# Turning the result blocks back on VectorE for every batch, in a fused attention and mixer kernel

## The chip, the cores and the metric

The kernel runs on one core of a Trainium2 chip, in one launch. The metric is the device time of one execution in microseconds. Engines are named as the profile names them: PE (TensorE; PEld is its weight load), DVE (VectorE), ACT (ScalarE), POOL (GpSimd) and SP (SyncE, which here only issues DMAs). Each engine works through its own instructions in the order in which the program issues them.

## The reference

Two blocks in a row, all in float32. Attention with 8 batches, 8 heads, 576 positions and 64 columns a head keeps only the 32 largest scores of each row; the mixer then works on x of shape (8, 576, 512).

```python
def _attn_ref(q, k, v):
    scores = scale * np.matmul(q, k.transpose(0, 1, 3, 2))
    kth = np.partition(scores, -32, axis=-1)[..., -32:-31]
    scores = np.where(scores >= kth, scores, -1000000000.0)
    attn = np.exp(scores - np.max(scores, axis=-1, keepdims=True))
    attn = attn / (np.sum(attn, axis=-1, keepdims=True) + 1e-09)
    return np.matmul(attn, v)

def _moe_ref(x, U, V, w_ch1, w_ch2):      # x: the heads side by side
    h = x.transpose(0, 2, 1) @ U @ V
    u = x + h.transpose(0, 2, 1)
    return u + np.maximum(u @ w_ch1, 0.0) @ w_ch2
```

## The kernel before

**Attention.** Two heads form a pair; a batch has four pairs, and a pair is worked through in five chunks of query rows: four of 128 rows for each head, and one with the last 64 rows of both heads. A step `n` of the main loop stands for one chunk. `scores` (matmul L323, copies L351) runs one step ahead. `front` finds the 32 largest scores of each row on DVE: in rounds of MAX8 (L432, L436, L446, L463) and MATCH_REPLACE8 (L434, L458), which remove the eight largest each time. The first part of `front`, up to L446, is issued at the start of the step by `next(fronts[n])`; a later `next(here)` issues the first L458, and so on. ACT and POOL put the threshold into the scores (L485, L488, L491), and ACT takes the exponentials (L397).

The probabilities must be transposed before they meet v. From the middle of the second batch `blocks` does that: DVE turns 32x32 blocks (L518, tile `y`, one buffer), four DMAs take them to DRAM (L524, tile `away`), and a fifth brings them back in transposed order (L528, tile `PT`). `values` reads `PT` two steps later in L585. A smaller part goes through PE (L551). `load` fetches the next pair with 21 DMAs on SP (L247, L252, L276, L279, L280), and DVE turns it (L293).

**Mixer.** `mixed` makes `uT`, the transposed u of a batch, pair by pair. With the last pair of a batch it appends the generator `mlp(b)` to `fillers`. `mlp` goes over the 576 positions in two spans, of 320 and 256 columns. In each span the first layer runs over 16 blocks of hidden units (L656, Relu L668), the second over four blocks `c` of 128 output channels (L675, 16 matmuls each). The sum with u lands in `oT`, transposed: 128 channels by 320 or 256 positions. ACT copies it from PSUM (L690) and POOL adds u (L691); in the last batch DVE does both at once (L688).

**Order.** The order is written by hand (`manual_schedule`). `fill`, called eight times a step, takes as many matmuls from `fillers` as a share of work says (`due`). So the mixer of batch b runs between the attention steps of batch b + 1, and the mixer of the last batch runs alone at the end.

**Turning back.** `mlp` appends `turned_back(...)` for each `c` to the list `late` and calls it later: at the 13th matmul of the next `c` (`f == 12`), at the fifth block of the next span's first layer (`f == 4`), or, for the last one of the batch, when the generator is resumed after its last yield. The function has two ways. One turns `oT` with PE transposes into PSUM (L723), copies with ACT (L725, L727), and writes with one DMA (L729), or two where the span has the last 64 positions (L734). The other turns 32x32 blocks with one DVE instruction (L705) into the tile `ob` (two buffers), and writes each quarter of 32 channels with a DMA for each of the position groups (L710 twice, L715 where the span has the last 64 positions): 12 DMAs in the first span, 8 in the second. It writes pieces of 32 floats, 128 bytes; the first way writes pieces of 512 bytes. The second way is now taken in the last batch alone, and there not for the very last block.

Of the kernel before, what the change touches and what calls it, by code (L numbers as in the profile page):

```python
# [26 lines left out]
def kernel(  # L27
# [29 lines left out]
    B, H, S, D = q.shape  # L57
# [4 lines left out]
    NF, NC = F // P, C // P  # L62
# [32 lines left out]
    SPAN = ((0, 2 * P + TAIL), (2 * P + TAIL, S))  # L95
# [30 lines left out]
    def rows(t):  # L126
        return P if t < NT else TAIL
# [568 lines left out]
    def turned_back(b, chunks, lo, c, oT):  # L696


        def run():
            cs = slice(c * P, (c + 1) * P)  # L700
            if b == B - 1 and (lo, c) != (SPAN[1][0], NC - 1):

                w = sum(rows(t) for t in chunks)
                ob = mlpp.tile([P, 3 * P], F32, tag="ob", name="ob", bufs=2)
                nc.vector.transpose(ob[:, 0:w], oT[:, 0:w])  # L705
                for a in range(4):
                    cs = slice(c * P + a * BLK, c * P + (a + 1) * BLK)
                    ba = ob[a * BLK : (a + 1) * BLK]
                    for t in chunks[0:2]:
                        nc.sync.dma_start(  # L710
                            out[b, 0:MAIN, cs].rearrange("(m i t) c -> t i m c", i=BLK, t=NT)[t],
                            ba[:, OFF[t] - lo : OFF[t] - lo + P].rearrange("i (m c) -> i m c", c=BLK),
                        )
                    if NT in chunks:
                        nc.sync.dma_start(  # L715
                            out[b, MAIN:S, cs].rearrange("(m i) c -> i m c", i=BLK),
                            ba[:, 2 * P : 2 * P + TAIL].rearrange("i (m c) -> i m c", c=BLK),
                        )
                return
            tp = ps_t.tile([P, 3, P], F32, tag="tp", name="tp")  # L720
            for i, t in enumerate(chunks):
                n = rows(t)
                nc.tensor.transpose(tp[0:n, i, :], oT[:, OFF[t] - lo : OFF[t] - lo + n], ident)  # L723
            ob = mlpp.tile([P, 3, P], F32, tag="ob", name="ob", bufs=2)
            nc.scalar.copy(ob[:, 0:2], tp[:, 0:2, :])  # L725
            if NT in chunks:
                nc.scalar.copy(ob[0:TAIL, 2], tp[0:TAIL, 2, :])  # L727
            t = chunks[0]
            nc.sync.dma_start(  # L729
                out[b, 0:MAIN, cs].rearrange("(p t) c -> p t c", t=NT)[:, t : t + 2, :],  # L730
                ob[:, 0:2],
            )
            if NT in chunks:
                nc.sync.dma_start(out[b, MAIN:S, cs], ob[0:TAIL, 2])  # L734

        return run
# [195 lines left out]
```

## Time and profile before

| | |
|---|---|
| median of 3 runs | 1718.03 us (1717.31 to 1718.37) |
| the profiled execution | 1716.65 us, span in the profile 1714.9 us |
| granted TensorE clock, mean | 0.97 |
| busy, share of the span | PE 94%, DVE 87%, ACT 60%, POOL 55% |
| PE transposes of `oT` (L723) | 142, mean duration 273 ns |
| block transposes of `oT` on DVE (L705) | 7, 445 to 513 ns |
| DMAs to the output | 57 L729, 28 L734; 56 L710, 16 L715 |

The span falls in four parts. Up to about 300 us PE is less than full, with the first batches' exact top-32 search on DVE and the weights still arriving; up to about 400 us DVE is full; from there to 1561 us attention and mixer run together in a pattern that comes back every 193.8 us; the rest is the end of the second-to-last mixer and the last mixer on PE. A row of busy times counts overlapping instructions once. In a row of instructions the mean duration of a pipelined matmul is longer than the time by which it holds up the next one. An idle time is given in brackets with what ended it.

### The profile page before, as it was taken

To read this page: it belongs to the slowest core of one execution; us is meant where nothing else is said; L and a number is where in the kernel's file an instruction comes from. 1 tells how busy PE (TensorE), PEld (TensorE's weight loads), DVE (VectorE), ACT (ScalarE), POOL (GpSimd) and SP (SyncE) were. 2 spreads that over 40 slices of the span, in tenths; PEclk is the share of its full clock that TensorE was granted. 3 is DMA by queue.
4 is the path that set the end of the run, shared out by engine and by line. 5 is a ranking of instruction groups with operands and counts; after the bars stand their busy time and mean duration, and the time that the engine had idled before them with its cause. 6 is when DMAs were issued, how large, how long until landed. Compare 5 with 4: busy or idle time off the path is not lost.

```text
span 1714.9 us, 29637 instructions
## 1 busy us (share of the span) xinstructions
PE 1613.5 (94%) x9489; PEld 1219.8 (71%) x9489; DVE 1484.2 (87%) x4317; ACT 1023.3 (60%) x2582; POOL 944.9 (55%) x749
## 2 busy tenths in 40 slices
PE   4666799998999999999999999999999999999999
PEld 2444566787777877788677877788677877788777
DVE  7999989999999999999999999999999999992000
ACT  4888797665656556565656566565655566563100
POOL 4778578666555555565555555565555555552000
PEclk7777899999999999999999999999999999999999
DMA  3322322344444444444444444444444444432010
GB/s 87 95 84 84 84 78 61 77 123 122 108 112 112 117 117 106 112 116 114 115 109 111 119 112 108 114 113 114 111 108 120 118 108 114 106 93 71 3 16 13
DMA packets 275837, 167.37 MB, mean 98 GB/s; under 512 B 173920, under 2 KB 260192, under 8 KB 275680
## 3 DMA queue, kind: packets, MB, share of 16 engines
q1 hardware_dynamic: 274624, 165.20, 37.2%
q8 instruction: 75, 1.23, 0.3%
q14 instruction: 82, 0.67, 0.1%
q10 hardware_dynamic: 1056, 0.26, 0.1%
HBM read 101.42 MB, written 63.96 MB: 96 GB/s over the span
## 4 chain that ended last, share of the span: by engine, by line
PE 71%; DVE 19%; SPq 3%; ACT 2%; issue 2%; DMA 2%; POOL 1%; POOLq 0%; DVEq 0%; ACTq 0%
PE mm L656 27%; PE mm L675 21%; PE sc L323 8%; DVE upper L458 6%; PE O L585 6%; DVE m L463 6%; DVE first L446 2%; SPq L252 2%; PE tp L551 1%; PE O L571 1%; SPq L247 1%; PE up L631 1%; PE O L581 1%; PE tp L546 1%; DVE y L518 1%
## 5 line engine op out<-in xcount | busy, mean ns | idle before, releaser
L675 PE MATMUL mm<-hT,w 128*128 128x256 f32 (+1 forms) x2048 | 529.5, 407 | 0.0
L656 PE MATMUL mm<-uT,w 128*128 128x256 f32 (+1 forms) x2048 | 522.8, 407 | 0.0
L491 POOL TENSOR_TENSOR Ssb<-Ssb,E 128x576 f32<-128x576 f32 x271 | 379.2, 1417 | 246.2 <-ACT E L488 245.8
L656 PEld LDWEIGHTS mm<-uT,w 128*128 128x128 f32 x2048 | 380.0, 191 | 97.6 <-issue 2.6
L675 PEld LDWEIGHTS mm<-hT,w 128*128 128x128 f32 x2048 | 377.9, 191 | 93.0 <-issue 2.9
L463 DVE MAX8 m<-upper 128x8 f32<-128x304 f32 (+1 forms) x864 | 407.7, 508 | 3.6
L458 DVE MATCH_REPLACE8 upper<-m,upper 128x304 f32<-128x304 f32 (+1 forms) x576 | 285.7, 502 | 0.0
L390 POOL TENSOR_TENSOR lower<-Ssb 128x576 uint32<-128x576 uint32 (+1 forms) x135 | 174.3, 1291 | 147.2 <-ACT Ssb L351 51.0
L393 POOL TENSOR_TENSOR lower<-lower,upper 128x576 uint32<-128x576 uint32 (+1 forms) x135 | 174.3, 1291 | 112.2 <-DVE upper L392 104.7
L397 ACT ACTIVATE Ssb<-Ssb,nmax 128x576 f32<-128x576 f32 x286 | 221.5, 777 | 15.3 <-POOL Ssb L468 9.3
L668 ACT ACTIVATE hT<-mm 128x320 f32<-128x320 f32 (+1 forms) x256 | 105.1, 410 | 192.9 <-PE mm L656 191.0
L323 PE MATMUL sc<-qkT 64*128 64x288 f32 x1334 | 211.7, 441 | 8.6 <-ACT Ssb L358 7.8
L488 ACT ACTIVATE E<-Ssb,least 128x576 f32<-128x576 f32 x271 | 198.0, 769 | 5.2
L323 PEld LDWEIGHTS sc<-qkT 64*128 64x128 f32 x1334 | 116.3, 183 | 63.8 <-issue 24.2
L585 PE MATMUL O<-PT,va 128*64 128x128 f32 x2048 | 144.5, 285 | 3.3 <-DMA PT<-away 3.2
L518 DVE STREAM_TRANSPOSE y<-Ssb 128x512 f32<-128x512 f32 x208 | 134.5, 682 | 14.8 <-ACT Ssb L397 14.7
L351 ACT COPY Ssb<-sc 128x576 f32<-128x576 f32 x216 | 127.5, 643 | 32.6 <-PE sc L323 31.0
L688 DVE TENSOR_TENSOR oT<-uT,mm 128x320 f32<-128x320 f32 (+1 forms) x8 | 3.6, 454 | 144.5 <-PE mm L675 144.5
L585 PEld LDWEIGHTS O<-PT,va 128*64 128x64 f32 x2048 | 113.2, 140 | 19.7 <-DMA PT<-away 3.9
L432 DVE MAX8 upper<-lower 128x8 f32<-128x288 f32 x243 | 97.9, 439 | 23.2 <-POOL lower L393 21.2
L392 DVE TENSOR_TENSOR upper<-sc,Ssb 128x576 f32<-128x576 f32 (+1 forms) x135 | 92.0, 682 | 20.7 <-ACT Ssb L351 20.1
L458 DVE MATCH_REPLACE8 upper<-first,upper 128x304 f32<-128x304 f32 x243 | 109.8, 458 | 0.0
(91 smaller groups left out, 1878.7 us busy)
## 6 DMA issues: line engine op xcount, KB each, us to landing
away<-y SPq DMA_DIRECT2D x416, 128.0 KB, 2.4
PT<-away SPq DMA_DIRECT2D x104, 512.0 KB, 3.3
raw<-in_moe_w_ch_dram SPq DMA_DIRECT2D x32, 512.0 KB, 3.9
va<-in_v_dram SPq DMA_DIRECT2D x64, 128.0 KB, 2.2
out_dram<-ob SPq DMA_DIRECT2D x57, 128.0 KB, 2.0
ld<-in_q_dram SPq DMA_DIRECT2D x108, 64.0 KB, 2.6
ld<-in_k_dram SPq DMA_DIRECT2D x108, 64.0 KB, 2.3
ld<-in_q_dram SPq DMA_DIRECT2D x108, 8.0 KB, 2.2
```

Source lines behind the costliest of these rows:

```text
L323: nc.tensor.matmul(out, lhsT=qkT[half(h), 0, cols(t)], rhs=qkT[half(h), 1, lo:hi], start=True, stop=True,)
L390: nc.gpsimd.tensor_tensor(bottom, a.bitcast(U32), b.bitcast(U32), ALU.add)
L393: nc.gpsimd.tensor_tensor(bottom, bottom, top.bitcast(U32), ALU.subtract)
L397: nc.scalar.activation(E, chunk, AF.Exp, bias=nmax, scale=SCALE, accum_out=total)
L458: nc.vector.match_replace(nxt, ms[c], curs[c], NEG)
L463: nc.vector.max(ms[c], curs[c])
L488: nc.scalar.activation(gap, chunks[c], AF.Relu, bias=least[:, c : c + 1], scale=-WIDEN)
L491: nc.gpsimd.tensor_tensor(chunks[c], chunks[c], gap, ALU.subtract)
L518: nc.vector.transpose(y[:, :, h].rearrange("p r c j -> p c r j"), E2[:, a : a + MAIN].rearrange("p (c r j) -> p c r j", c=NT, r=4),)
L585: nc.tensor.matmul(O[half(h)], lhsT=va[:, h, j, :], rhs=PB[:, h, j] if shared(g, t) else PT[:, NT * h + j], start=False, stop=(j == NT - 1),)
L656: nc.tensor.matmul(ph[:, 0:w], lhsT=w1[:, cc, f * P : (f + 1) * P], rhs=uT[:, cc, lo:hi], start=(cc == 0), stop=(cc == NC - 1),)
L675: nc.tensor.matmul(po[:, 0:w], lhsT=w2[:, f, c * P : (c + 1) * P], rhs=hTs[f][:, 0:w], start=(f == 0), stop=(f == NF - 1),)
```

## The change

One condition in `turned_back`. The way over DVE is taken for every block of every batch, apart from the very last block of the last batch, which keeps the way over PE.

```diff
         def run():
             cs = slice(c * P, (c + 1) * P)
-            if b == B - 1 and (lo, c) != (SPAN[1][0], NC - 1):
+            if (b, lo, c) != (B - 1, SPAN[1][0], NC - 1):

                 w = sum(rows(t) for t in chunks)
                 ob = mlpp.tile([P, 3 * P], F32, tag="ob", name="ob", bufs=2)
                 nc.vector.transpose(ob[:, 0:w], oT[:, 0:w])
                 for a in range(4):
                     ...
                     for t in chunks[0:2]:
                         nc.sync.dma_start(...)
                     if NT in chunks:
                         nc.sync.dma_start(...)
                 return
             tp = ps_t.tile([P, 3, P], F32, tag="tp", name="tp")
```

`oT` is made as before: by ACT and POOL in the first seven batches, by DVE in the last.

## The prediction

> **What bounds the kernel now.** I read the page first, then busy time by windows. From about 400 us on the order repeats every 193.8 us, one batch. Columns: window, length, then busy us (count) of PE, PEld, DVE, ACT, POOL, granted clock, DMA share, GB/s.
>
> ```profile
> 304.00:434.00 130.00, 123.69 (x772) 97.78 (x769) 129.45 (x405) 80.12 (x208) 77.40 (x62) 0.97 0.42 109
> 970.00:1164.00 194.00, 192.73 (x1164) 147.17 (x1164) 184.42 (x565) 118.33 (x304) 111.90 (x89) 1.00 0.44 113
> ```
>
> In the steady batches PE is busy 192.73 of 194 us and DVE 184.42. PE's waits there (582 to 1551 us) are one line, once per batch:
>
> ```profile
> PE tp L723 <- POOL oT L691: 6.4, 5, 1.3
> ```
>
> So PE sets the pace, and the only thing it waits for is the last turn-back of a batch. In 304 to 434 it is the other way round: DVE has no gap (129.45 of 130) and PE waits for what DVE delivers. After 1561 us DVE has nothing left and PE sets the end alone.
>
> **What leaves PE.** I call one `run()` of `turned_back` a turn: 56 turns change, eight per batch (0 to 3 of three PE transposes, 4 to 7 of two), 140 transposes. Their price is not the row's mean (273 ns, pipelined), but the shift of the next matmul, in PE's timeline:
>
> ```profile
> 1087.46 0.49 PE L723 MATMUL tp<-ident,oT 128*128 128x128 f32 x3
> 1087.79 1.51 PE L675 MATMUL mm<-hT,w 128*128 128x320 f32 x5
> ...
> 1010.30 0.60 PE L675 MATMUL mm<-hT,w 128*128 128x256 f32 x2
> 1012.17 0.44 PE L723 MATMUL tp<-ident,oT 128*128 128x128 f32 x2 [1.27 <-POOL oT L691]
> 1012.45 1.78 PE L656 MATMUL mm<-uT,w 128*128 128x320 f32 x6
> ```
>
> Three transposes take 1087.79 - 1087.46 = 0.33 us, 0.11 each. Turn 7 holds L656 from 1010.73 (second L675 plus its 0.215 pitch) to 1012.45: 1.7 us. A steady batch frees 4 x 0.33 + 3 x 0.22 + 1.7 = 3.7 us of PE. ACT loses 56 copies of 0.373 and 28 of 0.258 us, 28 us in all; at 118 of 194 us it is not the bound and PE waits nowhere for it in a steady batch, so I count nothing (were ACT the cover of some stall that is due, this would be a gain of up to that stall).
>
> [...]
>
> **What DVE gets.** The last batch shows the price: L705 takes 445 to 513 ns, so a batch adds 4 x 0.51 + 4 x 0.45 = 3.8 us, and 184.4 + 3.8 = 188.2 fits under PE's new 190.1. But DVE is in order. A step starts with `next(fronts[n])` (up to L446); turn 7 comes in a `fill()` behind scores and L551, before `next(here)` issues L458. So the new transpose stands between L446 and L458, and its data are late:
>
> ```profile
> 1006.47 0.83 DVE L446 MAX8 first<-upper 128x8 f32<-128x304 f32 x2
> 1007.23 0.07 DVE L458 MATCH_VALUE_LOAD upper<-first,upper 128x8 f32 x1
> ...
> 1012.51 0.69 DVE L518 STREAM_TRANSPOSE y<-Ssb 128x512 f32<-128x512 f32 x1
> 1016.02 0.71 DVE L518 STREAM_TRANSPOSE y<-Ssb 128x512 f32<-128x512 f32 x1 [2.82 <-ACT Ssb L397]
> ...
> 1011.39 0.73 POOL L691 TENSOR_TENSOR oT<-oT,uT 128x256 f32<-128x256 f32 x1 [0.22 <-DVE upper L458]
> ```
>
> oT is there at 1012.12, DVE wants it at 1007.23. With 0.5 us of its own, DVE goes on at 1012.6, 5.4 us late. Queued behind are two rounds of MATCH_REPLACE8 and MAX8, then y (L518). Y's second half had waited 2.82 us for ACT; that gap swallows part, so y ends at 1013.8 + 5.4 = 1019.2 instead of 1016.7, 2.5 late. Y goes out and comes back as PT through SP (L524, L528), and L585 reads it:
>
> ```profile
> 1020.58 0.34 SPq L528 DMA_DIRECT2D PT<-away  x1
> 1025.67 1.09 PE L585 MATMUL O<-PT,va 128*64 128x128 f32 x16
> ```
>
> With the page's 3.3 us to landing PT is there at 1023.9, 1.8 us early. It will come 2.5 later and PE will ask 1.7 earlier: a stall of 2.4 us. The other seven turns find oT ready (turn 0: DVE at 1083.7, POOL done at 1079) and cost their 0.5 us, beneath gaps such as L392's 1.66 us.
>
> **What SP gets.** One or two DMAs per turn become 12 (turns 0 to 3) or 8. In the last batch 12 of them run from 1630.81 to 1636.57: 5.7 us, 0.475 each; 8 take 3.8. A batch adds 80 x 0.475 = 38 us of SP and removes 12 issues of 0.55, 7. Before, SP issues in the window 64 L524 at 0.43, 64 loads at 0.62, 16 L528 at 0.34, 20 for v at 0.54 and 12 outputs: 90 us, 8 between them, and waits 31 for away to land (L528). The sum goes from 129 to 160 of 194. In order, though, a burst delays what follows. The worst place is turn 3, behind a head pair's 21 loads:
>
> ```profile
> 1137.54 0.63 SPq L280 DMA_DIRECT2D vt<-in_v_dram  x1
> 1138.27 1.44 SPq L729 DMA_DIRECT2D out_dram<-ob  x1
> 1139.81 0.49 SPq L734 DMA_DIRECT2D out_dram<-ob  x1
> 1140.49 1.89 SPq L524 DMA_DIRECT2D away<-y  x4
> 1144.44 0.34 SPq L528 DMA_DIRECT2D PT<-away  x1
> 1152.88 1.09 PE L585 MATMUL O<-PT,va 128*64 128x128 f32 x16
> ```
>
> Turn 2's burst comes before the block ahead (away at 1120.5, burst over at 1122.3), so the loads start 1.8 late and end at 1140.0; the burst ends at 1145.7. Away is 5.2 us late against a margin of 1152.88 - 1144.44 - 3.3 = 5.1, and PE has gained 1.3: a stall of 1.4 us. The same sum at turn 0 (away 1091.0 to 1095.4; margin 1104.5 - 1095.0 - 3.3 = 6.2) and turn 1 (1102.3 to 1105.9; margin 5.1) leaves about 1 us each; turns 4 to 6 push by 3 at most against 6 to 7. Two buffers are asked in time: `ob` is free again when the burst two turns earlier has landed (10 us before at the least), and `y`, with one buffer, when away has landed, at turn 1 by 1110.0 for a y at 1110.6; half a microsecond more and DVE waits for what is over. The pieces shrink from 512 bytes to 128: in the last batch's bursts the DMA share is 0.14 to 0.18 beside 0.44 in a steady batch, and each lands in 1.5 us, so I charge only 0.3 us per batch for later landings. Its bounds: zero, and 2 us at each of the four blocks a batch with under 2.5 us to spare.
>
> [...]
>
> **The sum.** Steady batches (1 to 5): -3.7 + 2.4 + 1.4 + 0.3 = +0.4, five times: +2.0.
>
> Batch 0 turns back from 296 to 423. There DVE is the bound, so turns 1 to 3 lengthen the path by 3 x 0.53 = 1.6. Turn 3's burst (from 347.4) pushes away, PT and then the loads from 355.1 to 358.5; they landed at 367.0 for a DVE that took them at 368.2, so DVE loses some 0.7 more. PE takes over at 397.55, 2.3 late. It gains 0.7 at turns 4 to 6 and 2.4 at turn 7 (its wait of 2.14 and the pair), and loses 0.5 on a block that turn 5's burst makes late. DVE, 3.8 late with turns 4 to 6, comes to turn 7 at 422.4 (L446 was done at 418.6), finds oT at 424.2, goes on at 424.7, and y is 5.7 late where PE has 1.2 to spare (PT issued at 440.0, L585 at 444.4) and is itself 0.25 early: a stall of 4.7. In all 2.3 - 0.7 - 2.4 + 0.5 + 4.7 = +4.4; bounds 0 (all in slack) and +9 (each term twice).
>
> Batch 6: turns 0 to 3 free 1.3 us, but the last PT lands at 1561.0, just as L585 starts, so PE only waits longer there. Turns 4 to 7 lie behind it: 6 x 0.11 + 1.5 = 2.2 us gained. Tail unchanged.
>
> Sum: 2.0 + 4.4 - 2.2 = +4.2 on 1716.65, the profiled execution (span 1714.9 plus 1.75 outside): 1720.9. The median of the runs is 1.4 higher, 1718.03, so 1722.2.
>
> **Rivals.** *PE keeps its gain.* The bursts stay in their margins and batch 0 costs 2: 5 x (-3.7 + 2.4) + 2 - 2.2 = -6.7, 1711. For it: DMA share 0.44, margins of 5 to 7 us behind loads. Against: the margins at turns 1 and 3 come out at 1 us or none. Without any stall it would be 7 x 3.7 = -26, 1692; the L446/L458 order excludes that.
>
> *SP becomes the bound*, the case that is clearly slower. Place: second layer of the first span, 55 us a batch with four bursts of 5.7. It decides when away and PT land 1 us later each: blocks with 1.6 to 2.4 us to spare then stall by some 1 us, four a batch, 4 x 6 batches = 24 on the small case, 1742. For it: PT landings up to 5.4 us in the trace. Against: the last batch's bursts land in 1.5 us at a 0.18 share.
>
> *DVE as the bound*: 188.2 + a 5 us wait at turn 7 = 193, nothing spare; gaps that do not close add 1 us a batch, +5 on the forecast, 1727, inside the range.
>
> **How the numbers follow.** Forecast (losses at turn 7 and turn 3 eat the gain) 0.54, PE keeps its gain 0.24, SP 0.22. A measurement of this kernel tells about 0.2% (3.4 us) from no change. The forecast's +4.2 lies just past that: of its 0.54 I put 0.33 slower, 0.19 within, 0.02 faster; of the second 0.20 faster, 0.04 within; the third is slower. That is 0.22, 0.23 and 0.55. The range 1710 to 1740 cuts off the far ends of both rivals.
>
> **What would show it.** L723 down to 2 per run, PE's L723 wait gone; DVE idle 3 to 5 us before L705 once a batch, by POOL oT L691; new PE waits of 1 to 2.5 us, L585 on PT, once or twice a batch; period near 194. Wrong if PE waits nowhere (then 1711 or less), or if L585 waits at four or more blocks a batch.

## The result and the profile after

The changed kernel takes 1739.68 us (median, 1737.49 to 1741.05) against 1718.19 for the kernel before on the same chip: a ratio of 1.0125, 95% interval 1.0107 to 1.0142. It is slower. The profiled execution took 1739.59 us, 22.9 more than the one before, with a span of 1737.4. PE is busy 92% of the span instead of 94%, DVE 87% as before. The times further down are medians of a run's executions; in two of the runs one execution was far longer than the others of the same kernel (2127.3 and 5579.27 us), and it is left out.

I measure the pattern at the L585 that follows turn 7, which stands once in every batch. Before, it starts at 444.4, 638.2, 831.9, 1025.7, 1219.4 and 1413.2 us, 193.8 apart. After, at 452.05, 648.7, 846.3, 1046.9, 1241.5 and 1437.0: periods of 196.6, 197.6, 200.7, 194.5 and 195.5. So the 22.5 us by which the span grew are 7.7 up to the end of batch 0, 16.1 in batches 1 to 5, and -1.3 behind them. The windows of the changed kernel, three whole batches (columns as in the prediction):

```profile
846.00:1047.00 201.00, 194.77 (x1142) 148.09 (x1143) 187.83 (x575) 115.53 (x293) 112.06 (x89) 0.97 0.44 109
1047.00:1241.00 194.00, 190.22 (x1140) 145.20 (x1140) 185.98 (x572) 114.93 (x292) 111.31 (x88) 1.00 0.46 113
1241.00:1437.00 196.00, 190.28 (x1142) 145.28 (x1142) 187.44 (x574) 115.47 (x293) 111.94 (x89) 1.00 0.45 112
```

Two things are to be seen. PE's work is down to 190.2 where the granted clock is 1.00, but the windows are 4 to 6 us longer than that: PE waits. And in the longest one PE is busy 4.5 us more with as many instructions, at a granted clock of 0.97: it runs slower for part of the time. The table of waits, 434 to 1570 us, has PE's only line and the first of DVE's (us in total, times, longest):

```profile
PE O L585 <- DMA PT<-away: 27.7, 17, 3.3
DVE ob L705 <- POOL oT L691: 16.2, 5, 3.3
```

PE's L723 wait is gone. L585 waits for PT instead, and DVE waits 3.2 us once a batch for the `oT` of turn 7. The timeline at one turn 7, with DVE, POOL, SP and PE one below the other:

```profile
1028.78 0.84 DVE L446 MAX8 first<-upper 128x8 f32<-128x304 f32 x2
1032.86 0.45 DVE L705 STREAM_TRANSPOSE ob<-oT 128x256 f32<-128x256 f32 x1 [3.24 <-POOL oT L691]
...
1038.49 1.29 DVE L518 STREAM_TRANSPOSE y<-Ssb 128x512 f32<-128x512 f32 x2
...
1032.10 0.72 POOL L691 TENSOR_TENSOR oT<-oT,uT 128x256 f32<-128x256 f32 x1 [0.22 <-ACT oT L690]
...
1031.41 7.80 SPq L710 DMA_DIRECT2D out_dram<-ob  x16
1039.80 1.75 SPq L524 DMA_DIRECT2D away<-y  x4
1043.70 0.34 SPq L528 DMA_DIRECT2D PT<-away  x1
...
1046.94 1.09 PE L585 MATMUL O<-PT,va 128*64 128x128 f32 x16 [2.20 <-DMA PT<-away]
```

DVE is done with L446 at 1029.6 and stands until POOL has made `oT` at 1032.8; y (L518), away and PT come late by it, and PE stands 2.2 us. SP is through with the bursts of turns 6 and 7 at 1039.2, before y is ready at 1039.78, so here DVE sets the time and not SP.

The other place is turn 3, behind the 21 loads. SP, then PE, and below them the DVE instruction that makes y, in the last of the steady batches:

```profile
1332.69 0.90 SPq L710 DMA_DIRECT2D out_dram<-ob  x2
...
1338.42 1.83 SPq L524 DMA_DIRECT2D away<-y  x4
1342.35 0.34 SPq L528 DMA_DIRECT2D PT<-away  x1
1342.74 0.63 SPq L247 DMA_DIRECT2D ld<-in_q_dram  x1
...
1349.92 1.43 SPq L252 DMA_DIRECT2D ld<-in_k_dram  x1
...
1356.50 0.64 SPq L280 DMA_DIRECT2D vt<-in_v_dram  x1
1357.24 1.11 SPq L710 DMA_DIRECT2D out_dram<-ob  x2
...
1362.66 0.43 SPq L715 DMA_DIRECT2D out_dram<-ob  x1
1363.19 2.20 SPq L524 DMA_DIRECT2D away<-y  x4
1367.38 0.34 SPq L528 DMA_DIRECT2D PT<-away  x1
...
1370.62 1.09 PE L585 MATMUL O<-PT,va 128*64 128x128 f32 x16 [2.93 <-DMA PT<-away]
...
1354.13 1.28 DVE L518 STREAM_TRANSPOSE y<-Ssb 128x512 f32<-128x512 f32 x2
```

Turn 2's burst (from 1332.69) pushes the away of the block ahead, that pushes the loads, turn 3's burst (1357.24 to 1363.1) comes behind them, and only then the four L524. DVE had y ready at 1355.4. Away starts 7.8 us later, and PE stands 2.93 us.

The third thing is the clock. Rows of 3.41 us each, as long as the half clock from 847.18 to 850.59 in them; the second number is the length, the third PE's busy time, and behind those of the five engines stands the granted clock:

```profile
843.77:847.18 3.41, 1.44 (x20) 1.09 (x18) 3.38 (x10) 0.98 (x2) 2.45 (x2) 1.00 0.48 162
847.18:850.59 3.41, 3.41 (x15) 2.02 (x12) 3.41 (x13) 1.71 (x4) 0.51 (x2) 0.50 0.58 146
850.59:854.00 3.41, 3.41 (x14) 2.38 (x14) 3.41 (x13) 1.34 (x3) 1.94 (x2) 1.00 0.73 195
1045.11:1048.52 3.41, 1.58 (x20) 1.35 (x22) 3.41 (x11) 1.25 (x3) 2.35 (x2) 1.00 0.58 182
1048.52:1051.93 3.41, 3.41 (x17) 2.26 (x14) 3.41 (x14) 1.71 (x4) 1.41 (x1) 1.00 0.36 98
```

The first row holds the stall of 1.98 us that ends at 846.26. In the row behind it PE is full but the granted clock is 0.50: 1.7 us of work lost. The fourth row holds the stall of 2.20 us that ends at 1046.94, and in the row behind it the clock is 1.00. Between 452 and 1437 us the changed kernel has three such stretches of 3.4 us and one of 6.8, each at the end of a stall of L585: 8.5 us lost. One more follows the stall that ends at 1437.0. The kernel before has none between 434 and 1570.

With that the account closes, batch by batch: -3.7 freed, plus the stalls (4.9, 5.6, 6.0, 4.3, 5.2), plus the half clock (1.7, 1.7, 5.1, 0, 0) gives +2.9, +3.6, +7.4, +0.6, +1.5; measured are +2.9, +3.8, +6.9, +0.8, +1.7.

### The profile page after: what moved, and what is told of

Its sections match the earlier page's. It is cut to its first block, busy times and chain, and to the rows that moved or that the text cites. A ratio compares the mean times of both kernels' runs of the same rounds, so it can differ in the third digit from the quotient of the medians.

```text
span 1737.4 us, 29816 instructions
## 1 busy us (share of the span) xinstructions
PE 1606.6 (92%) x9349; PEld 1211.1 (70%) x9349; DVE 1505.4 (87%) x4373; ACT 1001.2 (58%) x2498; POOL 944.6 (54%) x749
## 4 chain that ended last, share of the span: by engine, by line
PE 56%; DVE 28%; DMA 6%; SPq 4%; ACT 2%; POOL 2%; issue 2%; DVEq 0%; POOLq 0%
PE mm L675 21%; PE mm L656 18%; DVE upper L458 9%; DVE m L463 8%; PE sc L323 7%; PE O L585 5%; DMA PT<-away 3%; DVE first L446 3%; DVE lower L434 2%; DMA away<-y 2%; DVE upper L436 1%; DVE y L518 1%; DVE upper L432 1%; PE tp L551 1%; SPq L247 1%
## 5 line engine op out<-in xcount | busy, mean ns | idle before, releaser
L675 PE MATMUL mm<-hT,w 128*128 128x256 f32 (+1 forms) x2048 | 523.9, 407 | 0.0
L458 DVE MATCH_REPLACE8 upper<-m,upper 128x304 f32<-128x304 f32 (+1 forms) x576 | 285.9, 503 | 0.0
L323 PE MATMUL sc<-qkT 64*128 64x288 f32 x1334 | 216.5, 449 | 8.4 <-ACT Ssb L358 7.5
L585 PE MATMUL O<-PT,va 128*64 128x128 f32 x2048 | 145.9, 286 | 35.9 <-DMA PT<-away 35.8
L585 PEld LDWEIGHTS O<-PT,va 128*64 128x64 f32 x2048 | 114.0, 141 | 53.7 <-DMA PT<-away 26.2
L518 DVE STREAM_TRANSPOSE y<-Ssb 128x512 f32<-128x512 f32 x208 | 134.8, 684 | 10.2 <-ACT E L488 4.0
L594 ACT COPY XT<-O 128x128 f32<-128x128 f32 x128 | 33.9, 265 | 153.4 <-PE O L585 153.3
L458 DVE MATCH_REPLACE8 upper<-first,upper 128x304 f32<-128x304 f32 x243 | 109.9, 459 | 0.0
L434 DVE MATCH_REPLACE8 lower<-upper,lower 128x288 f32<-128x288 f32 x243 | 106.0, 443 | 0.0
```

The lines of the kernel that those rows point to most:

```text
L323: nc.tensor.matmul(out, lhsT=qkT[half(h), 0, cols(t)], rhs=qkT[half(h), 1, lo:hi], start=True, stop=True,)
L458: nc.vector.match_replace(nxt, ms[c], curs[c], NEG)
L518: nc.vector.transpose(y[:, :, h].rearrange("p r c j -> p c r j"), E2[:, a : a + MAIN].rearrange("p (c r j) -> p c r j", c=NT, r=4),)
L585: nc.tensor.matmul(O[half(h)], lhsT=va[:, h, j, :], rhs=PB[:, h, j] if shared(g, t) else PT[:, NT * h + j], start=False, stop=(j == NT - 1),)
L675: nc.tensor.matmul(po[:, 0:w], lhsT=w2[:, f, c * P : (c + 1) * P], rhs=hTs[f][:, 0:w], start=(f == 0), stop=(f == NF - 1),)
```

## The experiments

The first theory is the prediction's: two separate costs, turn 7's place in DVE's order and SP's bursts, each a stall of PE, to which the half clock is added. Its rivals: DVE's added work limits; the pieces of 128 bytes limit; or batch 0's late start is what matters.

**Turn 7 alone is moved.** The last turn of a batch is called after the step's last L458, not before its first.

```diff
-        late.pop()()
+        held.append(late.pop())
...                                # in the step, after the last next(here)
+        while held:
+            held.pop(0)()
```

> Only the last turn of each batch (turn 7) is moved: it is issued at the end of the step, after y, instead of between L446 and L458. DVE still does all turns, SP still writes the bursts. Theory (each steady batch loses a stall of 2 to 2.6 us at the block behind turn 7, one of 2.2 to 3.3 at the block behind turn 3's burst, and 1.7 us at half clock after some of these, against 3.7 gained): DVE's wait in front of L705 (16.2 us from 434 to 1570) is gone, so is PE's stall of 2 us at the block after it, five times, one of 1.3 in batch 0, and about half of the clock dips: 12 to 17 us less than the changed kernel, 1723 to 1728. Rival (DVE's or SP's total work sets the period, the place of the wait does not matter): 1737 to 1741. The stall behind turn 3's burst stays in both.

Measured: 1720.11 us, ratio 1.001 (1.000 to 1.002), 3 us below my range. PE's wait, and the window of a batch:

```profile
PE O L585 <- DMA PT<-away: 16.5, 10, 2.9
801.00:996.00 195.00, 191.42 (x1140) 146.04 (x1136) 186.86 (x572) 115.23 (x293) 111.41 (x89) 0.99 0.45 112
```

The stall behind turn 7 is gone in every batch (PT is there 1.2 to 1.4 us before L585). What is left is the one behind turn 3, 2.6 to 2.9 us each, and half clock behind four of those five. DVE does the same work as in the changed kernel, so this is a matter of order: 19.6 us of the 21.5 hang on where one instruction stands, together with its eight DMAs, which move with it.

**Few DMAs.** All turns stay where the change puts them, but SP has one or two DMAs for each, in pieces of 512 bytes. The kernel leaves out putting the 32x32 blocks into their places in the output.

```diff
+                if b < B - 1:
+                    t = chunks[0]
+                    nc.sync.dma_start(
+                        out[b, 0:MAIN, cs].rearrange("(p t) c -> p t c", t=NT)[:, t : t + 2, :],
+                        ob[:, 0 : 2 * P].rearrange("p (t c) -> p t c", t=2))
+                    if NT in chunks:
+                        nc.sync.dma_start(out[b, MAIN:S, cs], ob[0:TAIL, 0:P])
+                    return
```

> DVE does all turns as in the change, but in batches 0 to 6 the turned block is written with the one or two DMAs of the old way (512-byte pieces, so rows and columns of the output are not put into their places); the bursts of 12 and 8 are gone, the last batch is unchanged. Theory: the stalls behind turn 3's burst (2.2 to 3.3 us a batch, 15 with the small ones at other blocks) go, of batch 0's loss some 4, and the clock dips that follow them (5): 1714 to 1720; the stall behind turn 7 stays at about 2 us a batch. Rival (DVE: the wait at turn 7 and 27 us more work set the pace, bursts are hidden): 1735 to 1741.

Measured: 1714.99 us, ratio 0.9985 (0.9976 to 0.9995). PE's wait:

```profile
PE O L585 <- DMA PT<-away: 12.3, 7, 2.2
```

Now it is the other way round: the stall behind turn 3 is gone, and the one behind turn 7 stands in every batch with 2.1 to 2.2 us, with half clock behind three of the five. The two costs are separate, as the theory has it. This run alone can't tell the number of DMAs from the size of their pieces, since both change; a later one does.

**The bursts without the DVE work.** PE turns as before the change, and the results go out in 12 or 8 DMAs of 128-byte pieces.

```diff
...                                # against the kernel before: behind PE's transposes and ACT's copies, b < B - 1
+                for a in range(4):
+                    for i in range(2):
+                        nc.sync.dma_start(...)   # 32 channels of one position group
+                    if NT in chunks:
+                        nc.sync.dma_start(...)   # 32 channels of the last 64 positions
```

> The old way with PE transposes and ACT copies in batches 0 to 6, so DVE does as much as before, but each block is written in 12 or 8 DMAs of 128-byte pieces (a right output). Theory: SP's bursts alone, PE gains nothing: the block behind turn 3 stalls by some 1.4 us a batch (its margin is 1.3 larger than in the change), 0 to 3 in batch 0, PE's wait at turn 7 stays: 1722 to 1732. Rival (bursts do nothing by themselves): 1717 to 1719.

Measured: 1766.3 us, ratio 1.0282 (1.0264 to 1.0299). That is far above my range. The waits, 434 to 1570 us, and SP behind the loads:

```profile
PE O L585 <- DMA PT<-away: 34.1, 22, 4.4
DVE y L518 <- DMA away<-y: 22.6, 14, 3.3
...
1378.85 1.01 SPq L734 DMA_DIRECT2D out_dram<-ob  x2
1379.96 0.50 SPq L739 DMA_DIRECT2D out_dram<-ob  x1
...
1384.87 0.47 SPq L739 DMA_DIRECT2D out_dram<-ob  x1
1385.44 1.98 SPq L524 DMA_DIRECT2D away<-y  x4
```

This burst is longer than the change's: it runs from 1378.85 to 1385.4, 6.5 us instead of 5.8, as its issues cost more each (a pair 1.01 to 1.07 us and a single one 0.47 to 0.50, instead of 0.90 and 0.43 to 0.44 behind a first pair of 1.11). The stall behind turn 3 is 3.5 to 4.4 us instead of 2.2 to 3.3, and y's single buffer, which the prediction had seen half a microsecond from its limit, is past it: DVE waits 22.6 us for away to land (2.6 in the changed kernel). Without PE's gain, the period is 202.4.

**The same with 11 DMAs.** To see whether SP's lateness or the number of pieces sets that, the last 64 positions go out in pieces of 32, 32 and 64 channels.

```diff
+                    for u, v in ((0, 32), (32, 64), (64, P)):
+                        nc.sync.dma_start(out[b, MAIN:S, c * P + u : c * P + v], ob[0:TAIL, 2, u:v])
```

> As the run with TensorE turns and bursts of 12 and 8 DMAs, but the tail pieces are written in three DMAs of 32, 32 and 64 channels instead of four: 11 DMAs in a burst of the first span, 8 in the second. Theory (the time goes by SP's lateness behind the loads, with a stall for each tenth of it): the burst falls from 6.5 to about 5.8 us, the stall behind turn 3 from 3.5 to 4.4 us to under 3, and the time to 1740 to 1755. Rival (the time goes by the count of small pieces in the DMA engines, not by SP's order): pieces as many as before, 1762 to 1768.

Measured: 1748.24 us, ratio 1.0174 (1.0155 to 1.0193). PE's wait for PT:

```profile
PE O L585 <- DMA PT<-away: 16.2, 10, 3.7
```

One DMA less in a first-span burst takes 18.1 us off the time, as PE's wait for PT falls from 34.1 to 16.2 us and DVE's for away from 22.6 to 10.4. The pieces of that burst are a twentieth fewer only, so their number is not what sets the time. The stall behind turn 3 is still 2.2 to 3.7 us, where I had expected less than 3. The place behind the loads is a margin. Here it is used up, and the twelfth issue of each such burst is paid by PE, with 17.9 us of waits in all.

**Batch 0 left to PE.** `b > 0` is added to the changed condition; batches 1 to 6 are as in the change.

> The change for batches 1 to 7 only; batch 0 is turned by PE as before. Theory: batch 0's loss, 7.7 us to 452 us in the changed kernel's trace, is gone and does not come back later: 1730 to 1734. Rival (what batch 0 loses is waiting that later batches would have anyway): 1737 to 1741.

Measured: 1739.78 us, ratio 1.0123 (1.0106 to 1.0140): nothing won, as the rival had it, and not the 1730 to 1734 of my theory. At the L585 behind turn 7 of batch 0 this kernel is at 445.2, 7 us ahead of the changed one; then it loses them:

```profile
PE O L585 <- DMA PT<-away: 32.3, 16, 4.5
642.00:844.00 202.00, 194.61 (x1142) 148.09 (x1143) 188.09 (x575) 115.48 (x292) 112.11 (x89) 0.97 0.44 109
```

Periods are 196.7, 202.0, 200.2, 197.0 and 197.7. Each batch has a third stall of 0.9 to 1.6 us, at the block behind turn 1, and the stalls are 6.4 us a batch instead of 5.2; the half clock takes 11.9 us instead of 8.5.

**Batch 0 alone.** The reverse: the change in batch 0 and in none of batches 1 to 6.

```diff
-            if b == B - 1 and (lo, c) != (SPAN[1][0], NC - 1):
+            if b in (0, B - 1) and (b, lo, c) != (B - 1, SPAN[1][0], NC - 1):
```

> VectorE turns the blocks of batch 0 and, as in the kernel before, of the last batch; batches 1 to 6 use TensorE. My theory (batch 0's turns cost 5 to 8 us by the block after turn 7, and a kernel that TensorE bounds from there on can't make that up): 1722 to 1726, with the pattern of the kernel before, 193.8 us a batch, from 640 us on. Rival (a late start is made up in later batches, and that is why leaving batch 0 on TensorE won nothing): 1717 to 1720.

Measured: 1723.84 us, ratio 1.0036 (1.0023 to 1.0048). PE's waits and a window:

```profile
PE tp L723 <- POOL oT L691: 6.4, 5, 1.3
PE O L585 <- DMA PT<-away: 1.1, 1, 1.1
798.00:992.00 194.00, 192.73 (x1164) 147.20 (x1162) 184.42 (x565) 118.49 (x306) 111.50 (x88) 1.00 0.43 113
```

The pattern of before is back, with its old wait, and the delay stays to the end: 6.6 us at the last L585. So batch 0's cost is real where PE is the bound. In the changed kernel it is hidden: a PE that starts earlier waits more for PT.

**Both costs taken out.** Turn 7 later, as in the first run, and few DMAs, as in the second; the placing of the 32x32 blocks is left out here too.

> VectorE turns all blocks, turn 7 comes after the step's last L458 instead of before the first, and the results of batches 0 to 6 go out with one or two plain DMAs a turn (the 32x32 pieces are not put in their places in the output). Left out: the placing of the pieces. My theory (two costs, turn 7's order and SP's bursts, each a stall of PE with a half-clock stretch behind some of them): no wait of L585 over 1.5 us is left in the steady batches, no half clock, the period is PE's own work less 3.7 us, 190.1 to 190.8, so 5 x -3.2 = -16 in batches 1 to 5, -2 at the end, and +2 in batch 0: 1698 to 1704. Rival (VectorE's added work of 3.8 us a batch limits, whatever its order): PE goes on waiting for what VectorE delivers, the period stays at 192.5 or more, 1712 or above.

Measured: 1697.96 us, ratio 0.988 (0.9859 to 0.9901). A batch:

```profile
790.00:980.00 190.00, 190.00 (x1141) 145.20 (x1140) 186.56 (x573) 115.47 (x293) 111.86 (x89) 1.00 0.46 115
```

PE is busy 190.00 of 190.00 us at full clock. Nothing else is left, and the two costs nearly add up: singly their removal took 19.6 and 24.7 us off, together 41.7. The freed 3.7 us a batch arrive in full when neither stall stands in the way.

**A version with everything in place.** Turn 7 later; batch 0 on PE; in batches 1 to 6 the 512 first positions of both spans are gathered in one tile, so that a channel block goes out with 8 DMAs instead of 20, in the same pieces of 128 bytes.

```diff
-            if (b, lo, c) != (B - 1, SPAN[1][0], NC - 1):
+            if b > 0 and (b, lo, c) != (B - 1, SPAN[1][0], NC - 1):
...                                # turn 7 as in the first run; below: for 0 < b < B - 1; ow is half of a tile for two channel blocks
+                    nc.vector.transpose(ow[:, t * P : (t + 2) * P], oT[:, 0 : 2 * P])
+                    if NT in chunks:
...
+                        nc.vector.transpose(ob[:, 0:TAIL], oT[:, 2 * P : 2 * P + TAIL])
...
+                    for a in range(4):
...                                # cs, ba: the 32 channels of a
+                        if NT in chunks:
+                            nc.sync.dma_start(
+                                out[b, MAIN:S, cs].rearrange("(m i) c -> i m c", i=BLK),
+                                ob[ba, 0:TAIL].rearrange("i (m c) -> i m c", c=BLK))
+                        else:
+                            nc.sync.dma_start(
+                                out[b, 0:MAIN, cs].rearrange("(m i t) c -> i t m c", i=BLK, t=NT),
+                                ow[ba].rearrange("i (t m c) -> i t m c", t=NT, c=BLK))
```

> Nothing left out. Batch 0 is turned on TensorE as in the kernel before; in batches 1 to 6 VectorE turns the blocks, turn 7 comes after the step's last L458, the blocks of 512 positions of both spans are gathered in one tile and go out with four DMAs in the second span, the last 64 positions with four in the first: 8 DMAs a channel block instead of 20, with the same pieces of 128 bytes. Theory (SP's bursts and turn 7's order are all the cost): bursts of 4 leave every margin, no wait of L585 over 1.5 us in a steady batch, period 190 to 191.5, 1698 to 1708. Rival (the pieces of 128 bytes, not SP's count of DMAs, make PT late): stalls as in the run with turn 7 alone moved, 1716 to 1724.

Measured: 1694.55 us, ratio 0.9862 (0.9846 to 0.9877), 3 us below my range. PE's wait, a window, and SP's issues of one turn in each span:

```profile
PE O L585 <- DMA PT<-away: 0.3, 1, 0.3
975.00:1165.00 190.00, 190.00 (x1142) 145.22 (x1140) 186.77 (x577) 115.50 (x292) 111.86 (x89) 1.00 0.47 115
...
808.63 2.97 SPq L723 DMA_DIRECT2D out_dram<-raw  x4
887.68 1.94 SPq L718 DMA_DIRECT2D out_dram<-ob  x4
```

A turn's burst is now 2 to 3 us. The pieces are the small ones of the change, and no stall comes of them.

**The same with batch 0 on DVE.** There the bursts of 12 and 8 stay.

> As the run with gathered DMAs and batch 0 on TensorE, but batch 0 too is turned by VectorE, with its 12 and 8 DMAs a turn as in the changed kernel. Theory (batch 0 is bound by VectorE and its bursts fall before PE's blocks, so its cost stays): 4 to 8 us above that run, 1703 to 1715. Rival (what is lost in batch 0 is made up in the slack of later batches, as the run with batch 0 alone on TensorE suggested): within 2 us of it.

Measured: 1699.91 us, ratio 0.9894 (0.9879 to 0.9910), 5.4 us above the run before it, as the theory had it, though 3 us below my range, with the same pattern behind batch 0:

```profile
792.00:982.00 190.00, 190.00 (x1141) 145.19 (x1140) 186.75 (x577) 115.46 (x293) 111.84 (x89) 1.00 0.46 115
```

## Why the prediction was right, and where it was small

The sign is right, and so are the two places where PE stalls. The size is not: the sum gave 1722.2, which is 17.5 us short, +4.2 against +21.5. That 1739.68 still lies in the range, 0.3 us inside its upper end (one execution, 1741.05, lies beyond it), is partly luck: that end comes from the rival of SP as the bound (1742), and most of the miss is a cost that the sum does not have. The period, expected near 194, is 197.0 us in the mean. By its steps:

- **-3.7 us a batch leaves PE: right.** With both stalls away the period is 190.1 us (L585 at 785.0, 975.1, 1165.1, 1355.2 in the gathered version) against 193.8.
- **Turn 7, +2.4: right.** The stall is 2.0 to 2.6 us in the five batches, 2.2 in the mean, with DVE idle 3.24 us before L705 as forecast (3 to 5). Moving the one turn takes it away.
- **Turn 3, +1.4: mis-sized.** It is 2.2 to 3.3 us, 2.7 in the mean, and two of its terms are off. "Away is 5.2 us late" is 7.8 in the batch shown, 7.2 to 8.9 in the five: turn 2's burst pushes the away ahead of the loads by 2.85 us (y done at 1335.57, L524 at 1338.42) and not by 1.8, and the loads take 14.4 us instead of 13.5 (1124.70 to 1138.17 before), mostly by one L252 of 1.43. "PE has gained 1.3" came to nothing: from the end of y to where PE would have begun L585 there are 12.3 to 12.8 us in the changed kernel and 12.4 before. With both put right the step gives 7.9 (the mean) - 5.1 = 2.8 us. Had the gain been there, the stall would have been 4.
- **Later landings, +0.3: right in size.** Stalls at all other blocks add up to 1.4 us in five batches.
- **What the sum left out: the clock.** I priced a stall at its length. The half clock behind a stall takes 1.7 us more where it lasts 3.41 us, and twice that in the one place where it lasts 6.82: 8.5 us in batches 1 to 5, 60% of the 14.1 us by which these batches (+16.1 instead of +2.0) missed the forecast; the rest is turn 3's 6.7, less 1.1 that turn 7 stayed below its term.
- **Batch 0, +4.4: too small,** with +7.7 in the changed kernel, +6.6 when done alone and 5.4 as the difference of the last two runs' medians (7.7 at the last L585 of their traces). Where PE takes over the delay is 3.7 us (L585 at 401.3 instead of 397.6; forecast 2.3), and it grows to 7.7 by turn 7. Of that 1.7 us are again the clock: over 400 to 455 us it is 0.91 instead of 0.94. The sum was mixed otherwise than the trace: the stall behind turn 7, priced at 4.7, is 1.3 (at 452.05), and the L585 at 431.48 waits 1.59 us, where the sum has 0.5 for one late block.
- **Batch 6, -2.2:** from the last attention block (L585 at 1585.9 instead of 1561.0) to the end of the span the delay falls from 24.8 to 22.5, that is -2.3. The blocks ahead of it, counted at nothing, cost about 1 us with the half clock at 1437.7.

The rivals. *PE keeps its gain* (1711) is what the kernel would do if the bursts stayed in their margins, and the run with few DMAs, 1715, is that case. *SP becomes the bound* (1742) came near the time but not by its mechanism: L585 does not wait at four blocks a batch by about 1 us, it waits at two by 2 to 3.3, and at others by less than 0.5. In the run at 1766.3 us, with bursts 0.7 us longer, it does begin: other blocks wait too, by 0.3 to 2.1 us. *DVE as the bound* is out: in the gathered version DVE is busy 186.8 of 190 us and PE waits for nothing.

What stays open is why a PE that is 7 us ahead after batch 0 loses all of it. What fits: in the changed kernel PT of the blocks behind turns 0 and 1 lands 0 to 0.6 us ahead of L585 (the prediction left 1 us there), so a PE that is earlier against SP has to wait there. No run takes that margin apart by itself, and how much of the loss is the half clock, which follows some stalls and not others, was not separated either.

## What to carry to other kernels

Work that leaves a bounding engine is worth its pitch there only if nothing new stands in an in-order queue ahead of what that engine waits for: follow the moved instruction to its place in the new engine's order, and every DMA to its place in the issuing queue, and add up the delays of all bursts ahead of a tight transfer, not only of the nearest. Here 3.7 us a batch left PE, and they arrived in full, 190 us instead of 193.8, with both stalls out of the way. Price a stall with the clock that the trace shows behind it: here one of 1.98 us was followed by 3.41 us at 0.50, which is 1.7 us more. And before giving such a change up, try its parts: here the order of one instruction and the number of DMAs turned +21.5 us into -18.3, and with batch 0 left to PE into -23.7.

## What the runs showed of the hardware

**The half clock.** From 452 to 1570 us the changed kernel's granted clock is 0.50 in five stretches and 1.00 between them: 3.41 us from 580.9, 649.2, 847.2 and 1437.7, and 6.82 us from 976.9. Each stands at the end of a stall of L585: of 2.29 us (ending at 580.29), 2.56 (648.68), 1.98 (846.26), 2.12 (1436.99) and 3.31 (977.64). Behind the other five stalls of about 2 us or more, of 2.96 us (780.04), 2.20 (1046.94), 2.17 (1175.23), 2.00 (1241.48) and 2.93 (1370.62), the clock stays at 1.00. So the length of a stall alone does not tell whether half clock follows it, and no run was made to find what does. In the kernel before, which has no stall of L585 from 434 to 1570 us and waits of up to 1.3 us at L723, the clock is 1.00 all through.

**Small pieces and issues.** On SP an issue to the output costs 0.43 to 0.48 us in the changed kernel (1357.24 to 1363.1 for twelve, with a first pair of 1.11), and that count, not the pieces, was the cost here: with 128-byte pieces in 8 DMAs a channel block the DMA share is 0.47, with 512-byte pieces 0.46, and the period is 190 us with both.
